# Two tokens of a head per partition for chunks 0 and 1 of a retention layer with an MLP behind it

## The chip, the core and the metric

The kernel runs on one core of one Trainium2 chip. Its time is the device time of one execution in microseconds (us); several runs are made and the median is given. The core has five engines that run their own instruction lists in order and wait for each other through semaphores: PE (matrix products, with a separate queue of weight loads, PEld), DVE (vector), ACT (scalar functions), POOL (GpSimd) and SP (only issues DMAs here). ACT and POOL issue DMAs too. A DMA is cut into packets that 16 DMA engines carry.

## The reference

q, k and v have 4 batches, 8 heads, 768 tokens and 64 dimensions, all float32. The first half is a linear attention with one decay per head, the second a two-layer MLP with a tanh GELU:

```python
for t in range(S):
    state = gamma * state + k[t] (outer) v[t]        # per batch and head, 64 x 64
    y[t] = scale * q[t] @ state
x = y.transpose(0, 2, 1, 3).reshape(B * S, H * D)    # 3072 x 512
out = gelu_tanh(x @ w_in) @ w_out                    # w_in 512 x 2048, w_out 2048 x 512
```

## The kernel before, in words

Tokens are cut into six chunks c of 128 (`C`), and each chunk is worked on for the four batches b. The recurrence is done chunk by chunk as matrix products in fp16:

- `load1` (L100) brings one 128 x 512 float32 tile of q, k or v for (c, b): partition = token, and along the row the 64 dimensions of each of the eight heads, so that a row is eight packets of 256 bytes. `prep1` (L184) turns it into fp16, q and k times a decay.
- `mm_T`/`ev_T` (L222, L234): PE transposes q and k of a head pair (eight 128 x 128 transposes), ACT or DVE copies them out of PSUM as `qkT`.
- `mm_A`/`ev_A` (L247, L261): scores A = k q^T, eight products of 64 x 128 tiles, two of them at a time in the upper and lower half of the array; DVE multiplies two 128 x 512 banks with `mask` and writes `a_sb` in fp16.
- `mm_yc`, `mm_yi`, `ev_Y` (L268, L285, L298): y from the old state `st` (64 x 64 tiles, none in chunk 0) plus y from A and v (128 x 64 tiles), copied to `xT`.
- `mm_s`/`ev_S` (L307, L321): k^T v (128 x 64 tiles), added to the state `st`.
- The MLP of a chunk: `moe1`/`moe1_two` (L416, L421) multiply `xT` with w_in into one of two PSUM banks "h", and ACT applies GELU. `moe1_two` makes two of the 16 blocks of 128 hidden columns for part of the tokens (t0 to t1). For chunk 0 the second layer is `moe2` (L432); from chunk 1 on it is `units_w` (L518), which works with sums of the weights (`w_sums`, L469) and of the hidden values (`g_sums`, L476).

PSUM has eight banks: two with tag "h", two "o" and four "att" (L217), each taken in turn. Weights come by POOL's DMA queue (`load_w_in` L378, `load_w_out` L386), in four parts each, and are converted to fp16 on the way.

The order of everything is written out by hand. From L607 stands the opening: the loads (issued from SP and ACT, L134 to L144, L607, L608, L615), products of zeros (`spin`, L153) that fill PE's waiting, and the attention of chunk 0 for batches 0 to 2, before the first MLP product (L662, `moe1_two(0, 0, *t01)`, for the tokens of batches 0 and 1). POOL's list is: the k preparations, w_in part 0, k of batch 2, w_in parts 1 to 3, k and q of batch 3, w_out (L611 to L638). Chunk 1's loads are held back by two small POOL copies (`hold`, L683 and L689), which write into the tile that the load will fill. Then `run` (L714) interleaves the 16 units of the second layer of chunk 0 with the attention of chunk 1, and the next `run` (L734) the first layer of chunk 1 with the rest of it; the number before each entry is the unit after which it is issued. Chunk 2's loads (`load(2)`, L733, 16 DMAs for q alone, L113) stand on SP behind the output stores of batches 0 to 2 of chunk 0, which `ev_O` (L447) issues.

Of the kernel before, what the change touches and what calls it, by code (L numbers as in the profile page):

```python
# [9 lines left out]
F16 = mybir.dt.float16  # L10
F32 = mybir.dt.float32
AF = mybir.ActivationFunctionType
ALU = mybir.AluOpType
# [3 lines left out]
def kernel(  # L17
# [30 lines left out]
    cst_np = np.concatenate([qdec, kdec, gst, tri], axis=1).astype(np.float32)  # L48
# [17 lines left out]
    OQ, OK, OG, OT = 0, H, 2 * H, 2 * H + NHP  # L66
# [3 lines left out]
    cst = const.tile([128, 192], F32)  # L70
# [34 lines left out]

    def load_blk(nm, c):
# [27 lines left out]
    nc.sync.dma_start(out=cst[:, :OT + 128], in_=cst_h.ap())  # L134
    load1(nc.scalar, "q", 0, 0)
    load1(nc.sync, "k", 0, 0)
    load1(nc.scalar, "v", 0, 0)
    nc.sync.dma_start(out=iden, in_=iden_h.ap())
    load1(nc.sync, "q", 0, 1)
    load1(nc.scalar, "k", 0, 1)  # L140
    load1(nc.sync, "v", 0, 1)
    load1(nc.sync, "k", 0, 2)
    load1(nc.sync, "q", 0, 3)
    load1(nc.sync, "v", 0, 3)  # L144
# [19 lines left out]
    mask = const.tile([128, 2, NHP, 128], F32, name="mask")  # L164
    for j in range(2):
        for hp in range(NHP):
            nc.vector.tensor_scalar(
                out=mask[:, j, hp],
                in0=cst[:, OT:OT + 128],
                scalar1=float(1.0 / g128[2 * hp + j]),  # L170
                scalar2=None,
                op0=ALU.mult,
            )

# [9 lines left out]
    def prep1(eng, nm, c, b):  # L184
# [14 lines left out]
        h16[nm, c, b] = t  # L199

# [46 lines left out]
    def mm_A(c, b):  # L247
        t = qkT[c, b]
# [12 lines left out]
    def ev_A(c, b):  # L261
        ps = pss.pop(("A", c, b))
        for j in range(2):
            s = att.tile([128, NHP, 128], F16, tag=f"a{j}", name=f"a_sb{j}")
            nc.vector.tensor_tensor(out=s, in0=ps[j], in1=mask[:, j], op=ALU.mult)  # L265
            a_sb[c, b, j] = s

# [336 lines left out]
    half = 2 * C  # L604


    load1(AC, "q", 0, 2)  # L607
    load1(AC, "v", 0, 2)  # L608
    spin(14)
    prep1(VE, "q", 0, 0)  # L610
    prep1(PO, "k", 0, 0)  # L611
    prep1(AC, "v", 0, 0)
    mm_T(0, 0)
    ev_T(0, 0, AC)
    load1(AC, "k", 0, 3)  # L615
    prep1(VE, "q", 0, 1)
    prep1(PO, "k", 0, 1)
# [5 lines left out]
    prep1(AC, "v", 0, 1)  # L623
    spin(2)
    mm_yc(0, 0, "o")
    mm_yi(0, 0)
    mm_s(0, (0,), "o")
    ev_Y(0, 0, AC)
    prep1(VE, "q", 0, 2)

    load_w_in(0)
    prep1(PO, "k", 0, 2)
    for i in range(1, 4):
        load_w_in(i)
    prep1(PO, "k", 0, 3)
    prep1(PO, "q", 0, 3)
    for i in range(NO):
        load_w_out(i)  # L638
    mm_A(0, 1)
    ev_A(0, 1)  # L640
    spin(3)
    mm_T(0, 2)
    ev_T(0, 2, AC)
    spin(2)
    mm_yc(0, 1, "o")
    mm_yi(0, 1)
    mm_s(0, (1,), "o")
    ev_Y(0, 1, AC)
    prep1(AC, "v", 0, 2)
    spin(2)  # L650
    mm_A(0, 2)
    ev_A(0, 2)
    ev_S(0, (0,), AC)
    prep1(AC, "v", 0, 3)
    ev_S(0, (1,), AC)
    spin(6)
    mm_T(0, 3)
    ev_T(0, 3)


    t01, t2, t3 = (0, half), (half, half + C), (half + C, 2 * half)
    moe1_two(0, 0, *t01)  # L662
    mm_A(0, 3)
    ev_A(0, 3)
    mm_yc(0, 2, "o")
    mm_yi(0, 2)
    mm_s(0, (2,))
    ev_Y(0, 2, AC)
    moe1_two(0, 1, *t01)
    ev_S(0, (2,))  # L670
    moe1_two(0, 0, *t2)
    moe1_two(0, 1, *t2)
    mm_yc(0, 3, "o")
    mm_yi(0, 3)
    mm_s(0, (3,))
    ev_Y(0, 3)
    ev_S(0, (3,))
    moe1_two(0, 2, *t01)
    for fp in range(2):
        moe1_two(0, fp, *t3)  # L680
    moe1_two(0, 2, half, 2 * half)

    hold("q", 1, 0, w_out_sb[2][0:1, 0, 0:1])  # L683
    for fc in range(6, NF):
        moe1(0, fc)
        if fc in (8, 10):
            load1(AC, "v", 1, (fc - 8) // 2)
        if fc == 11:
            hold("q", 1, 0, g_tile(0, 10)[0:1, 0, 0:1])  # L689
# [8 lines left out]
    def preps(c, b):  # L698
        prep1(VE, "q", c, b)
        prep1(PO, "k", c, b)  # L700
        prep1(AC, "v", c, b)

    load1(SY, "q", 1, 0)
    load1(SY, "k", 1, 0)
    load1(SY, "q", 1, 1)
    load1(SY, "k", 1, 1)
    load1(SY, "q", 1, 2)
    load1(SY, "k", 1, 2)
    load1(SY, "q", 1, 3)
    load1(SY, "k", 1, 3)  # L710
    load1(AC, "v", 1, 2)
    load1(AC, "v", 1, 3)
    u = [units2(0, b, tag="ooho"[b]) for b in range(B)]
    run(  # L714
        [u[i % 3][i // 3] for i in range(12)] + u[3],
        {
            1: [(w_sums, 0)],
            2: [(w_sums, 1)],
            5: [(w_sums, 2)],
            7: [(w_sums, 3)],  # L720
            8: [(preps, 1, 0)],
            10: [(att_T, 1, 0), (preps, 1, 1)],
            11: [(att_AY, 1, (), "att", 1, (0,), None)],
            12: [(att_T, 1, 1), (preps, 1, 2)],
            13: [(att_AY, 1, (0,), "h", 1, (1,), AC)],
            14: [(att_T, 1, 2), (preps, 1, 3), (att_S, 1, 0)],
            15: [(att_AY, 1, (1,), "h", 1, (2,), AC), (att_T, 1, 3), (att_S, 1, 1)],
# [9 lines left out]
            for t in ((0, half), (half, 2 * half))  # L737
# [3 lines left out]
            1: [(att_AY, 1, (2,), "o", 1, (3,), VE)],  # L741
            3: [(att_S, 1, 2), (g_sums, PO, 1, 0, 4, 0, 1)],
            4: [(att_AY, 1, (3,), "o", 1, (), VE)],
            6: [(att_S, 1, 3)],
# [89 lines left out]
```

## Time and profile before

| | before |
|---|---|
| median of 3 runs | 211.7 us (211.4 to 211.85) |
| span of the profiled execution, first to last instruction | 209.7 us, so 2.0 us of the median lie around the span |
| PE busy | 200.6 us, 96% of the span; granted clock 0.998 |
| DVE, ACT, POOL busy | 104.1, 101.9 and 115.4 us |
| DMA | 33.19 MB in 124438 packets, 117952 of them under 512 bytes |
| first MLP product of chunk 0 | 16.7 us |
| first product of the second layer of chunk 0 | 32.9 us |
| first transposes of chunk 2 | 64.8 us |

The chain of waits is read backwards from the last instruction: each piece is what the next one waited for, or what stood before it on its engine. A stretch where it names only PE is one where nothing but PE's own work counts. The timeline lists instructions with their start, duration, engine and line, and in square brackets the idle time ahead of them.

### The profile page before, as it was taken

The page shows a single profiled execution, that of the slowest core. Times are in us where ns is not written, and L with a number is a line of the kernel's source. Part 1 is how long each engine was busy: PE and PEld are TensorE (multiplying, and loading weights), DVE is VectorE, ACT ScalarE, POOL GpSimd, SP SyncE. Part 2 cuts the span into 40 slices and gives each one's busy share as a digit, 9 for nine tenths or more (in the row PEclk, how much of TensorE's full clock was granted, in tenths as well). Part 3 has the DMA queues.
Part 4 walks back from the last instruction along what each step waited for, and adds up shares of the span by engine and source line. Part 5 has one row for each costly group of instructions (what it writes and reads, how often), then busy time and mean ns, then how long its engine had stood idle before and what let it go on. Part 6 is the DMA issues. An engine that isn't in the chain of part 4 may idle for free.

```text
span 209.7 us, 4776 instructions
## 1 busy us (share of the span) xinstructions
PE 200.6 (96%) x1928; PEld 132.0 (63%) x1928; DVE 104.1 (50%) x213; ACT 101.9 (49%) x182; POOL 115.4 (55%) x120
## 2 busy tenths in 40 slices
PE   7789999999998999999999999999999999999992
PEld 3347644456786878844688744678644788545881
DVE  4445153478734649703857630867432784053430
ACT  2474563144458615168745266643365811566311
POOL 0596001133099999249998299997499980200000
PEclk9999999999999999999999999999999999999999
DMA  7999999998899798799798698796970000500004
GB/s 168 287 253 207 206 205 222 273 269 215 157 220 233 110 179 163 110 313 177 124 219 128 124 340 131 125 207 99 206 251 0 0 3 0 203 0 0 0 28 177
DMA packets 124438, 33.19 MB, mean 158 GB/s; under 512 B 117952, under 2 KB 122432, under 8 KB 124416
## 3 DMA queue, kind: packets, MB, share of 16 engines
q1 hardware_dynamic: 108272, 21.09, 50.3%
q0 software_dynamic: 5456, 8.65, 17.4%
q10 hardware_dynamic: 10688, 3.15, 6.4%
q8 instruction: 15, 0.25, 0.4%
q14 instruction: 7, 0.06, 0.1%
HBM read 30.78 MB, written 6.29 MB: 177 GB/s over the span
## 4 chain that ended last, share of the span: by engine, by line
PE 81%; SPq 6%; ACT 4%; DMA 4%; DVE 2%; issue 1%; ACTq 1%; DVEq 0%
PE h_ps L398 35%; PE o_ps L536 29%; SPq L113 5%; PE o_ps L432 5%; PE a_ps L252 3%; PE y_ps L289 3%; PE y_ps L276 2%; DMA iden<-rr_ident 2%; DMA v<-in_v_dram 2%; PE qkT_ps L229 2%; PE spin_ps L156 1%; SPq L101 1%; PE s_ps L313 1%; ACT g L414 1%; ACTq L101 1%
## 5 line engine op out<-in xcount | busy, mean ns | idle before, releaser
L398 PE MATMUL h_ps<-xT,w_in 128*128 128x512 f16 (+2 forms) x488 | 87.4, 334 | 0.5 <-ACT g L414 0.5
L414 ACT ACTIVATE g<-h_ps 128x512 f16<-128x512 f32 (+1 forms) x98 | 57.5, 589 | 33.9 <-PE h_ps L398 33.5
L398 PEld LDWEIGHTS <-w_in 128*128 128x128 f16 x488 | 45.3, 97 | 37.4 <-issue 2.8
L467 POOL TENSOR_TENSOR s_g<-g 128x512 f16<-128x512 f16 x32 | 36.9, 1152 | 9.4 <-ACT g L414 9.4
L265 DVE TENSOR_TENSOR a_sb<-a_ps,mask 128x512 f16<-128x512 f32 x48 | 30.1, 682 | 23.1 <-PE a_ps L252 23.1
L536 PEld LDWEIGHTS <-s_g 128*128 128x128 f16 x320 | 30.2, 98 | 4.3
L536 PE MATMUL o_ps<-t_w,s_g 128*128 128x256 f16 x240 | 27.8, 273 | 0.0
L536 PEld LDWEIGHTS <-g 128*128 128x128 f16 x240 | 23.4, 98 | 3.6
L467 POOL TENSOR_TENSOR s_g<-s_g,g 128x512 f16<-128x512 f16 x16 | 18.4, 1153 | 1.3
L536 PE MATMUL o_ps<-w_out,g 128*128 128x256 f16 x160 | 18.6, 273 | 0.0
L467 POOL TENSOR_TENSOR s_g<-g,s_g 128x512 f16<-128x512 f16 x16 | 18.5, 1153 | 0.0
L193 POOL TENSOR_TENSOR k<-k,cst 128x512 f16<-128x512 f32 x8 | 8.3, 1044 | 17.3 <-DMA k<-in_k_dram 17.3
L569 POOL DMA_DIRECT2D out_dram<-o_sb x8 | 5.9, 737 | 20.3 <-DVE o_sb L467 16.8
L193 POOL TENSOR_TENSOR v<-v,cst 128x512 f16<-128x512 f32 x16 | 16.2, 1044 | 0.0
L238 DVE STREAM_TRANSPOSE qkT<-kT 128x512 f16<-128x512 f16 x12 | 8.1, 678 | 15.0 <-ACT kT L180 9.5
L565 ACT COPY o_sb<-o_ps 128x512 f32<-128x512 f32 (+1 forms) x5 | 2.7, 543 | 25.1 <-PE o_ps L536 25.1
L432 PE MATMUL o_ps<-w_out,g 128*128 128x512 f16 x64 | 14.8, 380 | 0.0
L305 DVE TENSOR_TENSOR xT<-y_ps,dec 128x512 f16<-128x512 f32 x16 | 10.3, 686 | 4.5 <-PE y_ps L289 4.5
L238 DVE STREAM_TRANSPOSE qkT<-q 128x512 f16<-128x512 f16 x16 | 11.0, 690 | 2.6 <-ACT q L180 2.5
L559 ACT COPY s_u<-o_ps 128x512 f32<-128x512 f32 (+1 forms) x6 | 3.1, 514 | 17.6 <-issue 9.9
L330 DVE SCALAR_TENSOR_TENSOR st<-st,cst,s_ps 128x128 f16<-128x128 f16 (+1 forms) x40 | 10.1, 313 | 2.0 <-PE s_ps L313 2.0
L156 PE MATMUL spin_ps<-zero 128*128 128x512 f16 x32 | 9.4, 429 | 1.2 <-DVE zero L148 1.2
(55 smaller groups left out, 185.3 us busy)
## 6 DMA issues: line engine op xcount, KB each, us to landing
k<-in_k_dram SPq DMA_DIRECT2D x22, 256.0 KB, 4.7
v<-in_v_dram SPq DMA_DIRECT2D x18, 256.0 KB, 4.0
q<-in_q_dram SPq DMA_DIRECT2D x64, 64.0 KB, 2.8
out_dram<-o_sb POOLq DMA_DIRECT2D x8, 512.0 KB, 5.2
kT<-in_k_dram SPq DMA_DIRECT2D x48, 64.0 KB, 2.7
w_in<-in_moe_w_in_dram POOLq DMA_DIRECT2D x4, 512.0 KB, 9.3
w_out<-in_moe_w_out_dram POOLq DMA_DIRECT2D x4, 512.0 KB, 14.7
v<-in_v_dram ACTq DMA_DIRECT2D x6, 256.0 KB, 5.5
```

The lines of the kernel that those rows point to most:

```text
L113: nc.sync.dma_start(out=t[p0:p0 + 32, :, a, :], in_=src[j, dd, t0:t0 + 32])
L156: nc.tensor.matmul(out=ps, lhsT=zero[:, 0:128], rhs=zero, start=True, stop=True)
L193: eng.tensor_tensor(out=t, in0=src, in1=cst[:, col:col + H].unsqueeze(2).broadcast_to([128, H, Dh]), op=ALU.mult,)
L238: nc.vector.transpose(out=t[:, i].rearrange("p hp t -> p (hp t)"), in_=blk16.pop((nm, c, b)).rearrange("p ha d -> p (ha d)"),)
L265: nc.vector.tensor_tensor(out=s, in0=ps[j], in1=mask[:, j], op=ALU.mult)
L305: nc.vector.tensor_tensor(out=x, in0=ps, in1=dec, op=ALU.mult)
L330: nc.vector.scalar_tensor_tensor(out=t[:, :, hp], in0=t[:, :, hp], scalar=cst[:, OG + hp:OG + hp + 1], in1=s_ps[:, :, hp], op0=ALU.mult, o ...
L398: nc.tensor.matmul(out=out, lhsT=w_in_sb[wi][:, kc, wr * 128:(wr + 1) * 128], rhs=xT[c][:, kc, t0:t1], start=(kc == 0), stop=(kc == NHP - ...
L414: nc.scalar.activation(out=out, in_=in_, func=AF.Gelu_apprx_tanh, scale=1.0)
L432: nc.tensor.matmul(out=ps[:, n0:n1], lhsT=g_sb[c, fc // 8][:, fc % 8, b * C:(b + 1) * C], rhs=w_out_sb[fc // (NF // NO)][:, fc % (NF // NO ...
L467: eng.tensor_tensor(out=out, in0=in0, in1=in1, op=op)
L536: nc.tensor.matmul(out=po, lhsT=lhs(c, lk, fp, a), rhs=rhs(rk, fp), start=(new and fp == 0 and (last or a == 0)), stop=(stop and fp == NP ...
```

## The change

For chunks 0 and 1 (`TP`) a partition holds tokens 2p and 2p+1 of one head, with p = 0 to 63 and the heads 0 to 3 in the lower, 4 to 7 in the upper 64 partitions. A row is then four packets of 512 bytes. Each load becomes two DMAs of 64 partitions (`load2`). What follows:

- `prep2` is two instructions of 128 x 256 instead of one of 128 x 512, for q and k. A transpose now gives, per token parity r, two heads times 64 tokens.
- A, the inner part of y, and S are made of 64 x 64 tiles: 16 products where there were 8, in an order (`QUADS`) that takes the four quarters of the array in turn. The part of y from the old state keeps its number. Each result lies in two banks, by half hh.
- In chunk 1 the state part and the inner part of y write to one bank from different row halves. So `mm_yc2` ends with an ACT copy of one element (`seen`) that waits for its last product, and the first product of `mm_yi2` waits for that copy.
- `ev_Y2` and `ev_S2` are two copies each (chunk 0), by half.
- The constants `cst` grow from 148 to 424 columns (74 to 212 KB), the mask of chunks 0 and 1 is made by four instructions of 128 x 256, and the mask for the later chunks is made over by `masks` in the MLP of chunk 1.
- The opening: ACT issues only q, v of batch 0 and k of batch 1, all else is on SP; the first w_in part goes ahead of k of batch 1 on POOL, and part 1 ahead of batch 2; the first MLP product comes after batch 1; the narrow units (one batch, 128 tokens) of the first layer are eight instead of four.
- Chunk 1: one hold instead of two; attention in pairs of batches (`att2`, `att_S2`), transposes from unit 7 on; the second layer of chunk 0 runs batches 0 and 1, then 2 and 3, all in "o" banks, so that the store of batch 2 is issued after unit 14.

```diff
+    def load2(eng, nm, c, b, halves=(0, 1)):
+        t = ld_tile(nm, c, b).rearrange("p (x j) d -> p x (j d)", x=4)
+        for hh in halves:
+            eng.dma_start(
+                out=t[hh * 64:(hh + 1) * 64],
+                in_=srcs[nm][b, 4 * hh:4 * hh + 4, c * C:(c + 1) * C, :].rearrange(
+                    "h (p r) d -> p h (r d)", r=2
+                ),
+            )
...
-    nc.sync.dma_start(out=cst[:, :OT + 128], in_=cst_h.ap())
-    load1(nc.scalar, "q", 0, 0)
...
+    load2(nc.scalar, "q", 0, 0)
+    nc.sync.dma_start(out=cst, in_=cst_h.ap())
+    load2(nc.sync, "k", 0, 0)
+    load2(nc.scalar, "v", 0, 0)
     nc.sync.dma_start(out=iden, in_=iden_h.ap())
+    load2(nc.scalar, "k", 0, 1)
+    load2(nc.sync, "q", 0, 1)
+    load2(nc.sync, "v", 0, 1)
+    for nm in "kqv":
+        load2(nc.sync, nm, 0, 2)
+    for nm in "kqv":
+        load2(nc.sync, nm, 0, 3)
...
+    QUADS = [(x, r, j, hh) for x in range(2) for r in range(2) for j in range(2) for hh in range(2)]
...
+    def mm_A2(c, b):
+        t = qkT[c, b]
+        ps = [bank("att", name=f"a_ps{j}") for j in range(2)]
+        for x, r, j, hh in QUADS:
+            nc.tensor.matmul(
+                out=ps[j][half(hh), 2 * x + r],
+                lhsT=t[half(j), 1, 2 * x + r, half(hh)],
+                rhs=t[half(j), 0, 2 * x:2 * x + 2, half(hh)],
+                start=True,
+                stop=True,
+            )
...
+    def mm_yc2(c, bs, tag):
+        ys = [bank(tag, shape=(128, len(bs), 2, 128), name=f"y_ps{hh}") for hh in range(2)]
...
+        seen = nc.scalar.copy(out=misc[0:1, 1:2], in_=ys[1][0:1, len(bs) - 1, 1, 0:1])
+        needs(seen, ins)
+        yc_last[c, bs] = seen
...
+    def mm_yi2(c, bs):
...
+            for x, r, j, hh in QUADS:
+                ins = nc.tensor.matmul(
+                    out=ys[hh][half(j), i, x],
+                    lhsT=h16["v", c, b][half(hh), 4 * x + 2 * j + r],
+                    rhs=a_sb[c, b, j][half(hh), 2 * x + r],
...
+                if behind is not None:
+                    needs(ins, behind)
...
+    def mm_s2(c, bs, ss=None):
+        if ss is None:
+            ss = [bank("att", shape=(128, len(bs), 2, 64), name=f"s_ps{hh}") for hh in range(2)]
...
+    def att2(c, bs, tag, ca, abs_, engs):
+        if bs:
+            mm_yc2(c, bs, tag)
+        for b in abs_:
+            mm_A(ca, b)
+        if bs:
+            mm_yi2(c, bs)
+            ev_Y2(c, bs, engs)
+        for b in abs_:
+            ev_A(ca, b)
...
+    def ys_mm(b):
+        zs = [bank("o", shape=(128, 512), name=f"z_ps{hh}") for hh in range(2)]
...
+        mm_s2(0, (b,), ss)
+        mm_yi2(0, (b,))
...
     spin(14)
+    prep2(VE, "q", 0, 0)
+    prep2(PO, "k", 0, 0)
+    load_w_in(0)
+    prep2(PO, "k", 0, 1)
+    prep2(AC, "v", 0, 0)
     mm_T(0, 0)
+    prep2(VE, "q", 0, 1)
+    ev_T(0, 0, VE)
     spin(3)
     mm_A(0, 0)
     ev_A(0, 0)
     mm_T(0, 1)
     ev_T(0, 1, AC)
+    spin(3)
+    ys_mm(0)
+    prep2(AC, "v", 0, 1)
+    load_w_in(1)
+    prep2(PO, "k", 0, 2)
+    prep2(PO, "q", 0, 2)
+    ev_Y2(0, (0,), (AC, AC))
+    ev_S2(0, (0,), AC)
+    spin(3)
+    mm_A(0, 1)
+    ev_A(0, 1)
+    mm_T(0, 2)
+    ev_T(0, 2, AC)
+    spin(3)
+    ys_mm(1)
+    load_w_in(2)
+    prep2(PO, "k", 0, 3)
+    prep2(PO, "q", 0, 3)
+    load_w_in(3)
     for i in range(NO):
         load_w_out(i)
+    ev_Y2(0, (1,), (AC, AC))
+    prep2(AC, "v", 0, 2)
...
+    moe1_two(0, 0, *t01)
     mm_A(0, 2)
     ev_A(0, 2)
+    ev_S2(0, (1,), VE)
+    moe1_two(0, 1, *t01)
     mm_T(0, 3)
+    ev_T(0, 3, VE)
+    prep2(AC, "v", 0, 3)
+    ys_mm(2)
+    ev_Y2(0, (2,), (AC, VE))
+    moe1_two(0, 2, *t01)
     mm_A(0, 3)
     ev_A(0, 3)
+    ev_S2(0, (2,), AC)
+    moe1_two(0, 3, *t01)
+    for fp in range(3):
+        moe1_two(0, fp, *t2)
+    ys_mm(3)
+    ev_Y2(0, (3,), (AC, VE))
+    ev_S2(0, (3,), VE)
+    moe1_two(0, 3, *t2)
+    for fp in range(4):
         moe1_two(0, fp, *t3)
...
-        [u[i % 3][i // 3] for i in range(12)] + u[3],
+        [u[b][i] for b0 in (0, 2) for i in range(4) for b in (b0, b0 + 1)],
         {
...
+            2: [(w_sums, 2)],
+            4: [(w_sums, 3)],
+            5: [(preps, 1, 0)],
+            7: [(att_T, 1, 0), (preps, 1, 1)],
+            9: [(att_T, 1, 1), (preps, 1, 2)],
+            10: [(att2, 1, (), "h", 1, (0, 1), None)],
+            11: [(att_T, 1, 2), (preps, 1, 3)],
+            13: [(att_T, 1, 3)],
+            14: [(att2, 1, (0, 1), "h", 1, (2, 3), (AC, VE))],
+            15: [(att_S2, 1, (0, 1))],
...
+            1: [(att2, 1, (2, 3), "o", 1, (), (VE, AC))],
+            3: [(att_S2, 1, (2, 3)), (g_sums, PO, 1, 0, 4, 0, 1)],
+            5: [(masks,)],
```

## The prediction

> **What bounds the kernel now.** The page first:
>
> ```profile
> PE 200.6 (96%) x1928; PEld 132.0 (63%) x1928; DVE 104.1 (50%) x213; ACT 101.9 (49%) x182; POOL 115.4 (55%) x120
> ...
> DMA  7999999998899798799798698796970000500004
> GB/s 168 287 253 207 206 205 222 273 269 215 157 220 233 110 179 163 110 313 177 124 219 128 124 340 131 125 207 99 206 251 0 0 3 0 203 0 0 0 28 177
> ```
>
> PE is busy for all but 9 us. The DMA engines are full from the second slice (5.2 us) to 45 us. Next the chain of waits, in order of time (start, us, what):
>
> ```profile
> 10.60 0.33 PE a_ps L252 x8
> 10.93 0.75 PE spin_ps L156 x3
> ...
> 13.18 0.50 ACT xT L180
> ...
> 14.90 1.40 PE spin_ps L156 x6
> 16.30 0.45 PE qkT_ps L229 x8
> 16.75 1.02 PE h_ps L398 x8
> ...
> 19.58 0.60 ACT g L414
> ...
> 22.32 0.60 ACT g L414
> ...
> 22.97 10.11 PE h_ps L398 x56
> 33.08 9.50 PE o_ps L432 x44
> ```
>
> Until 16.7 us the attention of the first batches runs at the pace of loads, ACT and DVE, and products of zeros fill PE. From there on PE alone counts: it stands still for 0.8 us at the two ACT pieces (0.4 us each between the products), 0.6 us ahead of the first transposes of chunk 2 (64.8 us), and hardly elsewhere. So there are two places to gain: an earlier first MLP product, and less PE work. There is much room to lose, because every new wait of PE behind 16.7 us counts in full.
>
> Why 16.7? The timeline of the opening (start, us, engine, line, operation, idle before):
>
> ```profile
> 7.87 1.04 POOL L193 TENSOR_TENSOR k<-k,cst 128x512 f16<-128x512 f32 x1 [1.24 <-DMA k<-in_k_dram]
> 8.75 1.29 DVE L265 TENSOR_TENSOR a_sb<-a_ps,mask 128x512 f16<-128x512 f32 x2 [0.86 <-PE a_ps L252]
> 8.85 0.92 POOL L379 DMA_DIRECT2D w_in<-in_moe_w_in_dram  x1
> ...
> 14.90 1.06 POOL L193 TENSOR_TENSOR q<-q,cst 128x512 f16<-128x512 f32 x1
> ```
>
> xT of batches 0 and 1 is ready at 13.7 (the ACT piece at 13.18). But w_in part 0, issued at 8.85, takes 7.8 us to land (the shortest of its four in the table of DMA issues), so 16.65; q of batch 3 is prepared at 15.96 and its transposes stand ahead too. In the trace's packet records the first packet of w_in starts at 13.1, when ACT's queue of loads has run dry.
>
> **Loads of chunk 0.** From 4 to 12 us the queues carry 283 to 289 GB/s, nearly all 256-byte packets. The packet records show 18.0 ns for 256 bytes and 84 ns for 2048 (chunk 0's stores). A line through both gives 27.4 ns for 512 bytes, so 288 x 36/27.4 = 378 GB/s (estimate). A half load writes 64 partitions, which no row shows; the nearest are the 64 KB loads of L113 to 32 partitions, at one per 0.53 us (128-byte packets), 124 GB/s. So 124 to 378; I take 340, near the upper end, since a 256-byte packet is nearer to 512 than L113's. Up to q of batch 1 there are 5 loads of 262 KB, cst 217 (74 before) and iden 33: 1.56 MB, from 1.8 us on, the first 0.5 us at 200 GB/s, so 6.6 us, and 0.6 us until DVE can start (as for q of batch 1 before): 7.2, as before (7.20). The bigger cst eats what the packets give.
>
> A page speaks against the change. The Trainium skill, "SBUF — State Buffer", section "Door 1: The DMA port swizzle (why [64,N] ≈ [32,N])", says that a transfer to 64 partitions reaches 8 of 16 ports and carries 196 to 218 GB/s, and that two such transfers side by side gain 6%. By that the 3.15 MB of chunk 0 would take 14.4 us instead of 10.9; no run here shows it.
>
> **First MLP product.** DVE: q of batch 1 7.2 to 7.9, then the copy of the transposes that was ACT's (0.69 on DVE, 1.0 on ACT): 8.6; before 8.26. A: 8.6 to 9.0; two mask products 1.29: 10.4. ACT copies the transposes of batch 1 from 9.6 to 10.6. y and S: 10.5 to 11.0; three zeros 0.7 (row 10.93); A of batch 1 11.7 to 12.0; masks to 13.5; y to 14.0; two ACT copies of 128x256 (0.38, as GELU's): **14.8**. In the same time w_in part 0: k of batch 0 lands at about 5.1 (5.58 before), its preparation 1.04, issue at 6.2, and 7.8 us as before: 14.0. It doesn't bind then. Gain 16.7 - 14.8 = 1.9 us, bounds 0 and 2.8 (chain pieces without the zeros).
>
> **From there to the second layer** (32.9 before, 16.2 us). The MLP itself is the same work: PE starts narrow products 56 ns apart, 216 ns for four times as many columns. But the transposes of batch 3 (0.45) and A of batch 2 (0.33), once ahead of 16.7, now stand behind. Each of A, y and S of chunk 0 has a change of tile shape on either side. In the trace's single records the step between the last product of one shape and the first of the next is 0.10 to 0.12 us longer; I count 0.11. One more there: 0.1. New waits: (1) y and S of batch 2 need both "o" banks, and DVE frees them with `ev_S2` of batch 1 behind the two masks of batch 2: A ends 1.3 us after the start of this part, masks 1.29, two copies about 0.55: 3.2, PE is there at 2.6: 0.6 us. (2) Eight narrow units of 0.45 us against GELU's 0.38 plus some 0.3 us of hand-over in two banks, after wide ones with 0.60: 0.4 at the first, as now, and about 0.6 over the rest. Sum 16.2 - 0.8 + 0.9 + 1.6 = 17.9 us. The second layer starts at 14.8 + 17.9 = 32.7: **-0.2 us**. The gain is handed back.
>
> **64x64 tiles.** The records show two-tile shapes (L252, L289, L276) starting pairs 3 ns apart, and the pairs 56 ns apart (128 columns); S pairs 32 ns. Four tiles at a time: 16 products in four steps of 56, as 8 in four pairs before: no cost. If only two go together, A, inner y and S of a batch cost 0.22 + 0.22 + 0.13 us more, over eight batches 4.6, some 3.4 of it behind 14.8. No row shows four; I take four, since rows and columns each pair freely. What is saved is shape changes: 25 in chunk 1 before, by the chain's order (A, y, S per batch), 10 after: 15 x 0.11 = **-1.65 us**.
>
> **New waits in chunk 1.**
> - Transposes of batch 3 (after unit 13) need q of batch 3, and DVE's list from the transposes of batch 1 on is copy, q, four masks, copy, q: 0.6 + 0.65 + 2.45 + 0.6 + 0.65 and 0.3 of hand-over, 5.25 us (rows: two masks 1.29, copy to next 0.60). PE's work in between is four units of 0.86, A 0.55, transposes 0.46: 4.45. **+0.8** (0.4 to 1.2).
> - S of batches 0 and 1 needs two "att" banks; all four hold A of batches 2 and 3, and DVE first copies y (0.6), then masks batch 2 (1.3), from 0.25 us after y: 2.15. PE comes at 0.97 (one unit). **+1.2** (0 to 1.3).
> - `seen`: the first has 0.45 us of A as cover and stands behind ACT's copy of o_ps (0.58): 0 to 0.1. The second stands behind a GELU (0.60) that starts when the unit ends, with only the 0.55 us of state products as cover: 0.25 + 0.6 + 0.2 + 0.05 - 0.55 = **+0.5** (an element costs ACT 0.20). Behind it in ACT's queue are one y copy and GELUs with slack.
> - SP: the store of batch 2 now waits for unit 14, about 50 us instead of 44; dec and the 16 q loads (10.6 us, 46.83 to 57.42 now) end near 62 and land near 64, when ACT wants them (63.1 before). That fits only because of the waits above; they share the time, so 0 here, up to 1.3.
> - `masks` is 1.17 us on DVE, which idles there: 0.
>
> Sum of chunk 1: -1.65 + 0.8 + 1.2 + 0.5 = +0.85, with -0.2 it is **+0.65 us**. Chunks 2 to 5 keep their work. The span would be 210.4; the 2.0 us between span (209.7) and median stay: 211.7 + 0.65 = **212.3**.
>
> **Rivals.**
> 1. *Faster.* DVE's waits vanish: bank and list order as I read them cost 1.0 instead of 2.6 us in chunk 1 and 0.8 less in the opening, loads near 378 GB/s start the MLP 0.3 us earlier: 212.3 - 1.6 - 0.8 - 0.3 = 209.6; half of it gives 211.0. For it: PE has next to no such gaps now. Against: the order of the lists is fixed, and DVE was already busy 4.43 of the 5 us from 45 to 50. 36%: 209.4 to 211.2.
> 2. *Clearly slower: w_in against the loads.* w_in now goes out at 6.2 while SP still has five to seven loads to bring, all in one queue. From 31 to 34 us the trace shows w_out beside ACT's v loads: packets one for one, about 150 per us of each, so a half-kilobyte queue gets 77 GB/s, 3.4 us per load. If w_in starts at 8.5 instead of with the queue dry, k and q of batch 3 are ready near 18 to 20, and their transposes stand in PE's list at 17: +1.5 to +3; with loads at some 200 GB/s, inside the bounds above, also batch 2 is late, +4 to +9. It decides from a load rate under about 280 GB/s or a w_in delay under 3 us. 22%: 213.5 to 219, middle 215.5.
> 3. *No gain in rate*: 512-byte packets at 288 GB/s delay q of batch 1 and everything to 14.8 by about 0.9 us: 213.2, inside my own case's upper part.
>
> **How the numbers follow.** Own case 42% (211.3 to 213.5, value 212.3), rival 1 36%, rival 2 22%. About 0.2% (0.4 us) is what a measurement tells from no change: faster is under 211.3, slower over 212.1. Same: the lower third of my case, 14%; slower 28 + 22 = 50%; faster 36%. The range leaves out the fastest tenth (under 209.8) and the slowest tenth (over 216.5); my own case alone is 211.3 to 213.5.
>
> **What would show it.** Right: first h_ps near 14.8, first o_ps of L630 near 32.7, PE gaps ahead of S (L424, about 1.2) and of the last transposes of chunk 1 (0.8) with DVE as releaser, 16 products of 64x64 in the time of 8. Wrong: GB/s in the second slice not over 290, the first h_ps waiting for w_in, a gap ahead of batch 3's transposes in the opening, A products starting 28 ns apart instead of 14.

## The result, and the profile after

The changed kernel takes 236.2 us (median of 4 runs, 233.0 to 236.9) against 211.8 for the kernel before on the same chip (4 runs, 211.4 to 213.8): a ratio of 1.107, 95% interval 1.098 to 1.117. The forecast was 212.3, its range 209.8 to 216.5. Some executions of a kernel run longer at a lower granted clock, and the ratios in this document leave those out while the medians in us do not, so that for e4 and e13 below the ratio goes with 218.3 and 226.3 us. The profiled execution has a span of 234.2 us, 24.5 more than before.

The page of the changed kernel, the rows that answer to those shown of before:

```profile
span 234.2 us, 5251 instructions
PE 209.9 (90%) x2138; PEld 136.3 (58%) x2138; DVE 109.3 (47%) x218; ACT 102.6 (44%) x190; POOL 118.0 (50%) x130
...
PEclk9857999958999999999999999997799999999999
DMA  6999799696077997989988989989983000040004
GB/s 169 210 229 235 114 196 177 196 224 184 4 186 113 195 217 92 179 138 273 190 125 164 164 236 202 136 169 160 139 166 148 3 0 3 0 179 3 0 0 179
```

PE has 24 us without work, 9 before. Where before the rate was 287 and 253 GB/s in the second and third slice it is now 210 and 229, and the granted clock falls in three places: in the opening, near 50 us and near 160 us. Those are the three places where PE waits. The chain of waits, in order of time (start, us, what), names the first two:

```profile
3.89 5.12 DMA q<-in_q_dram
...
12.75 8.57 DMA k<-in_k_dram
...
26.00 12.23 DMA w_out<-in_moe_w_out_dram
...
50.31 0.60 ACTq L124
50.96 0.60 ACT g L612
51.61 2.31 PE o_ps L630 x5
```

Before, the chain was PE from 22.97 us on; here it is loads, their issues and POOL up to 51. At 50.3 it shows something else: ACT issues a load, and only then the GELU that PE waits for. The last line shows a second price of a wait: five products in 2.31 us, 462 ns each (they start 427 ns apart), where the row shown of before has 44 in 9.50 (216 ns). Around the waits of PE the trace has its clock granted at half: from 10.3 to 20.5 us, from 47.8 to 54.7 and from 160.5 to 167.3. Not every long wait does this: in e8 below PE waits 3.3 us for one load and keeps its full clock.

The first product times on PE cut both executions into stages (us; the last column is what the forecast added for the stage):

| stage | before | after | change | forecast |
|---|---|---|---|---|
| start to first MLP product | 16.7 | 21.3 | +4.5 | -1.9 |
| to the second layer of chunk 0 | 16.2 | 18.4 | +2.2 | +1.7 |
| to the first MLP product of chunk 1 | 19.0 | 28.5 | +9.5 | +0.85, with the next row |
| to the first transposes of chunk 2 | 12.9 | 13.1 | +0.2 | in the row above |
| to the last product | 140.6 | 149.1 | +8.4 | 0 |

**The opening.** From the timeline of the changed kernel (start, us, engine, line, operation, idle before):

```profile
7.81 0.92 POOL L577 DMA_DIRECT2D w_in<-in_moe_w_in_dram  x1
...
10.21 1.22 POOL L252 TENSOR_TENSOR k<-k,cst 128x256 f16<-128x256 f32 x2 [1.48 <-DMA k<-in_k_dram]
...
14.61 1.18 POOL L252 TENSOR_TENSOR k<-k,cst 128x256 f16<-128x256 f32 x2 [2.42 <-DMA k<-in_k_dram]
16.62 1.18 POOL L252 TENSOR_TENSOR q<-q,cst 128x256 f16<-128x256 f32 x2 [0.83 <-DMA q<-in_q_dram]
```

Everything waits for loads: k of batch 1 is taken up at 10.2 (7.9 before), q of batch 2 at 16.6. By the packet records w_in part 0 starts near 9.8, and from 11 to 13 us, in half microseconds, it moves 130 to 203 GB/s while the loads of q, k, v move 6 to 78. The transposes of batch 2 stand ahead of the first MLP product on PE; they start at 17.3, when POOL has prepared the first half of q.

**Chunk 1.** What ACT waited for between 30 and 60 us in the changed kernel (us in total, times, longest):

```profile
ACT g L612 <- DMA q<-in_q_dram: 9.4, 1, 9.4
...
ACT g L612 <- DMA k<-in_k_dram: 2.2, 1, 2.2
```

Its list around the longer one (timeline of the changed kernel):

```profile
38.11 0.60 ACT L612 ACTIVATE g<-h_ps 128x512 f16<-128x512 f32 x1 [0.27 <-PE h_ps L596]
45.94 2.15 ACTq L124 DMA_DIRECT2D v<-in_v_dram  x2
48.14 0.60 ACT L612 ACTIVATE g<-h_ps 128x512 f16<-128x512 f32 x1 [9.44 <-DMA q<-in_q_dram]
```

A GELU reads nothing that a load brings. But the v loads of chunk 1 stand in ACT's list ahead of the last two GELUs, and their issue waits: the program has eight completion semaphores for the DMAs of SP and ACT, given out in turn, and an issue waits until the earlier DMA with its semaphore has landed. Those earlier ones are SP's q and k loads: the issue at 45.94 has the semaphore of the k load that SP issued at 42.67 and that landed at 45.92.

**The end.** SP's list before, then after, around the first loads of chunk 2 (L113, L138):

```profile
46.83 10.59 SPq L113 DMA_DIRECT2D q<-in_q_dram  x16
```

```profile
55.38 9.83 SPq L653 DMA_DIRECT2D out_dram<-o_sb  x3
...
65.78 9.71 SPq L138 DMA_DIRECT2D q<-in_q_dram  x16
```

The third store waits for unit 14, and with it all later loads: they start 15.5 us ahead of chunk 2's first transposes, before it was 18.0. SP then issues with no gap over 0.5 us up to kT of chunk 4 (128.6 to 140.7 us) and never makes it up. There was next to no room in that list: before, this kT landed at 119.8, 0.9 us ahead of its use. From the first of these loads to that landing it was 73.0 us before and 77.5 now; why the list itself takes longer is not shown. At chunk 4 POOL pays, and PE behind it (the timeline after; before, POOL began the same casts at 120.7 with no wait):

```profile
143.44 2.28 POOL L222 CAST kT<-kT 128x512 f16<-128x512 f32 x4 [6.24 <-DMA kT<-in_k_dram]
...
161.83 2.53 PE L734 MATMUL o_ps<-t_w,s_g 128*128 128x256 f16 x11 [4.16 <-POOL s_g L665]
```

### The profile page after: what moved, and what is told of

Its sections match the earlier page's. It is cut to its first block, busy times and chain, and to the rows that moved or that the text cites. A ratio compares the mean times of both kernels' runs of the same rounds, so it can differ in the third digit from the quotient of the medians.

```text
span 234.2 us, 5251 instructions
## 1 busy us (share of the span) xinstructions
PE 209.9 (90%) x2138; PEld 136.3 (58%) x2138; DVE 109.3 (47%) x218; ACT 102.6 (44%) x190; POOL 118.0 (50%) x130
## 4 chain that ended last, share of the span: by engine, by line
PE 62%; DMA 14%; POOL 10%; SPq 4%; DVE 3%; ACT 3%; issue 1%; ACTq 0%; POOLq 0%; DVEq 0%
PE h_ps L596 26%; PE o_ps L734 26%; POOL s_g L665 8%; DMA k<-in_k_dram 5%; DMA w_out<-in_moe_w_out_dram 5%; SPq L124 4%; DMA q<-in_q_dram 4%; PE o_ps L630 2%; PE y_ps L487 2%; PE y_ps L474 2%; DVE a_sb L329 1%; PE a_ps L315 1%; PE qkT_ps L290 1%; ACT g L612 1%; PE s_ps L511 1%
## 5 line engine op out<-in xcount | busy, mean ns | idle before, releaser
L596 PEld LDWEIGHTS <-w_in 128*128 128x128 f16 x512 | 46.6, 98 | 38.4 <-issue 4.2
L734 PEld LDWEIGHTS <-s_g 128*128 128x128 f16 x320 | 31.2, 101 | 11.3 <-POOL s_g L665 6.1
L734 PE MATMUL o_ps<-t_w,s_g 128*128 128x256 f16 x240 | 30.4, 287 | 5.6 <-POOL s_g L665 5.6
L734 PEld LDWEIGHTS <-g 128*128 128x128 f16 x240 | 23.4, 98 | 3.6
L630 PE MATMUL o_ps<-w_out,g 128*128 128x512 f16 x64 | 16.6, 402 | 6.2 <-ACT g L612 5.6
L252 POOL TENSOR_TENSOR k<-k,cst 128x256 f16<-128x256 f32 x16 | 9.8, 627 | 24.5 <-DMA k<-in_k_dram 24.5
L665 POOL TENSOR_TENSOR s_g<-s_g,g 128x512 f16<-128x512 f16 x16 | 18.4, 1153 | 1.3
L767 POOL DMA_DIRECT2D out_dram<-o_sb x8 | 5.9, 737 | 17.3 <-DVE o_sb L665 14.0
L630 PEld LDWEIGHTS <-g 128*128 128x128 f16 x64 | 6.1, 101 | 13.8 <-ACT g L612 6.6
L222 DVE COPY qkT<-qkT_ps 128x1024 f16<-128x1024 f16 (+1 forms) x10 | 5.8, 578 | 14.9 <-PE qkT_ps L290 14.9
L220 ACT CAST q<-q 128x512 f16<-128x512 f32 x16 | 9.5, 618 | 6.8 <-DMA q<-in_q_dram 3.7
L503 DVE TENSOR_TENSOR xT<-y_ps,dec 128x512 f16<-128x512 f32 x16 | 10.3, 686 | 4.5 <-PE y_ps L487 4.5
L182 PE MATMUL spin_ps<-zero 128*128 128x512 f16 x26 | 11.2, 596 | 1.2 <-DVE zero L174 1.2
```

Of the source, the lines that this page charges most:

```text
L182: nc.tensor.matmul(out=ps, lhsT=zero[:, 0:128], rhs=zero, start=True, stop=True)
L220: eng.copy(out=out, in_=in_)
L252: eng.tensor_tensor(out=t[:, 4 * x:4 * x + 4].rearrange("p (r j) d -> p j r d", r=2), in0=src[:, 4 * x:4 * x + 4].rearrange("p (j r) d -> ...
L503: nc.vector.tensor_tensor(out=x, in0=ps, in1=dec, op=ALU.mult)
L596: nc.tensor.matmul(out=out, lhsT=w_in_sb[wi][:, kc, wr * 128:(wr + 1) * 128], rhs=xT[c][:, kc, t0:t1], start=(kc == 0), stop=(kc == NHP - ...
L630: nc.tensor.matmul(out=ps[:, n0:n1], lhsT=g_sb[c, fc // 8][:, fc % 8, b * C:(b + 1) * C], rhs=w_out_sb[fc // (NF // NO)][:, fc % (NF // NO ...
```

## The experiments

Theories: **T1**, a load to 64 partitions is slow to write. **T2**, twice as many loads share eight completions. **T3**, w_in takes the queues from the loads. **T4**, SP's list is late behind the third store. **T5**, tiles and list order cost something of their own. **T6** was formed on the way: the issue of a load is what is slow. Each ratio is to the kernel before, run beside it, with its interval. The runs were made on four chips, where the kernel before took 211.8 to 213.0 us, so a difference between runs of two chips can be off by about 1 us. Waits of PE are taken from the starts of its products: the step to the next one, less its usual length.

**Load shape in the changed kernel.** `e1` takes two loads of 128 partitions with two columns each, `e2` one with all four (in the code below, a step and a slice of 4). They bring other data, four heads of 256 tokens in place of eight heads of 128, so that e1, e2 and the runs built on e2 (e8, e14, e15) do not compute the layer; only their time is read.

```diff
+        src = srcs[nm][b, 4 * c:4 * c + 4, 0:2 * C, :].rearrange("h (p r) d -> p h (r d)", r=2)
+        for s in range(0, 4, 2):
+            eng.dma_start(out=t[:, s:s + 2], in_=src[:, s:s + 2])
```

> The changed kernel, with the two loads of a tensor each over all 128 partitions and two of its four 512-byte columns, instead of over 64 partitions and all four. Number (two), size (128 KB) and packet size (512 bytes) of the loads stay, and so do order, waits and all work on the engines. The data are others (four heads of 256 tokens in place of eight heads of 128), so what is computed is not the reference; read for its time alone. Theory T1, a load to 64 partitions is slow (about 215 GB/s against 288): the lateness goes; loads of the opening at 280 GB/s or more, first MLP product at 15 to 17.5 us, transposes of chunk 2 at 64 to 67, time 211.5 to 215. Theory T2, the number of loads (eight completions in turn, twice as many of half the size): nothing changes, 234 to 237. Theory T3, w_in beside the loads: the first MLP product stays over 19 us, time 216 to 230.

> As the run with two wide loads, but one load of 256 KB per tensor, 128 partitions, 512-byte packets (other data, as there). T1: the same as the two wide loads, within 1 us. T2: only here the loss goes, 211.5 to 215 against 234 to 237 there. T3: first MLP product over 19 us in both.

Measured: e1 231.9 us, 1.090 (1.083 to 1.096); e2 227.7, 1.068 (1.061 to 1.074). Neither theory alone: full width brings 4, the smaller number another 4, and most of the loss stays. The gain lies in chunk 1, whose stretch of 28.5 us falls to 23.6 and 20.7. Up to the second layer neither gains (39.6 us in the changed kernel, 41.3 in e1, 40.2 in e2): e2's first MLP product comes at 16.0, but PE then waits for batch 3.

**Load shape in the kernel before.** `e3` cuts its loads by tokens, `e4` by heads:

```diff
+                eng.dma_start(out=t[64 * s:64 * s + 64], in_=src[64 * s:64 * s + 64])
```
```diff
+                eng.dma_start(out=t[:, 4 * s:4 * s + 4], in_=src[:, 4 * s:4 * s + 4])
```

> The kernel before, each load of q, k, v of chunks 0 and 1 cut into two of 64 partitions (tokens 0 to 63, 64 to 127), 256-byte packets as before. T1: the loads of chunk 0 fall from 288 to about 215 GB/s, first MLP product 3 to 4 us later, chunk 1 late as in the changed kernel: 218 to 232. T2: as slow as the run with two loads of four heads each, whatever that is. If both are 211 to 213, the slow loads belong to 512-byte packets and not to half loads.

> The kernel before, each load of q, k, v of chunks 0 and 1 cut into two of all 128 partitions and four heads each, 256-byte packets. T1: no change, 211 to 213. T2: the issue of each load waits for the one eight before it, of half the size: 216 to 232, as slow as the run with half partitions.

Measured: e3 225.0, 1.056 (1.050 to 1.062); e4 220.5, 1.025 (1.017 to 1.034). The old layout, with 256-byte packets, loses 12 us by nothing but half loads, and about half of that by their number alone. So 512-byte packets are not needed for a loss. But it is lost elsewhere: the first MLP product comes at 28.0 in e3 and 23.1 in e4 (16.7 before), and from the second layer on both run as before to 0.2 us, with chunk 1's half loads at 210 GB/s in e3. In e3's opening the loads still carry 247 GB/s from 3 to 12 us (280 before, to 9.5); what comes late is ACT's first conversion of v, at 12.0 instead of 6.7, behind ACT's own issues, and PE waits 5.5 us for the copy behind it. Windows of the changed kernel, of e1 and of e2 show why the load shape counts in chunk 1 (from:to, us, then busy times, clock, DMA share, GB/s; the stretches are loads of chunk 0 and of chunk 1):

```profile
3.00:9.50 6.50, 5.61 (x22) 2.04 (x20) 1.90 (x6) 2.00 (x3) 2.31 (x3) 1.00 1.03 223
40.00:50.00 10.00, 6.02 (x27) 2.36 (x24) 2.28 (x6) 0.60 (x1) 2.36 (x4) 0.89 0.73 201
```
```profile
39.00:47.00 8.00, 8.00 (x39) 3.58 (x37) 3.02 (x6) 1.78 (x4) 3.70 (x6) 1.00 0.82 230
```
```profile
3.00:9.50 6.50, 4.70 (x22) 1.81 (x20) 3.09 (x8) 1.44 (x3) 3.48 (x6) 1.00 1.16 298
38.00:46.00 8.00, 8.00 (x39) 3.63 (x37) 2.19 (x6) 2.26 (x5) 2.36 (x4) 1.00 0.97 277
```

In chunk 1 the rate falls 277, 230, 201, and the DMA share falls with it, 0.97, 0.82, 0.73: the engines are not slower, they have nothing to do. By the packet records a packet takes 27 ns (median) in all three. In the opening it is not so: there the share is 1.03 in the changed kernel, and from 8 to 10 us its packets take 39 to 45 ns. What fits chunk 1 is SP's own pace. Its very first loads have nothing ahead to wait for; SP's first k loads in the changed kernel, in e1 and in e2:

```profile
1.12 1.43 SPq L124 DMA_DIRECT2D k<-in_k_dram  x2
```
```profile
1.14 1.00 SPq L125 DMA_DIRECT2D k<-in_k_dram  x2
```
```profile
1.12 0.49 SPq L125 DMA_DIRECT2D k<-in_k_dram  x1
```

Two half loads take 1.43 us to issue, e1's two 1.00, e2's one 0.49. So an issue costs 0.5 us for 128 partitions, whether 128 or 256 KB, and about 0.66 for 64 (from one to the next in chunk 1). 131 KB per 0.66 us is 198 GB/s. That is T6.

**Order of the lists.** `e5` (T4), `e6` (T2) and `e7` (T3), each one edit:

```diff
-        eng = nc.sync if b < B - 1 else nc.gpsimd
+        eng = nc.sync if b < B - 2 else nc.gpsimd
```
```diff
-            load2(AC, "v", 1, fc - 13)
...
+        for b in (b0, b0 + 1):
+            load2(SY, "v", 1, b)
```
```diff
+    prep2(PO, "k", 0, 1)
     load_w_in(0)
-    prep2(PO, "k", 0, 1)
...
+    prep2(PO, "k", 0, 2)
+    prep2(PO, "q", 0, 2)
     load_w_in(1)
```

> The changed kernel with one edit: the store of batch 2 of chunk 0 goes out on POOL's queue, as that of batch 3 does, so that SP goes on to the loads of chunk 2 without waiting for unit 14. Theory T4 (SP's list of loads, put behind that store, runs late up to chunk 4 and makes POOL and PE wait at 157 to 166 us): the loads of chunk 2 start near 57 instead of 65.8 us, POOL's casts of kT of chunk 4 wait for nothing, the two gaps of PE ahead of chunk 3's second layer (1.6 and 4.3 us) and the slower clock behind them go, 8 us less: 227 to 229. If the late second half is only the opening's lateness carried on (T1), nothing changes: 235 to 237.

> The changed kernel with one edit: the loads of v of chunk 1 leave ACT's list and go out on SP, behind q and k of the same two batches. Theory T2 (a load's issue waits for the landing of the eighth load before it, and ACT's GELUs stood behind such an issue): the gaps of 3.6 and 2.6 us at 48.8 and 51.6 go, and the stretch from the first second-layer product of chunk 0 to the first product of chunk 1's MLP falls from 28.5 to about 23 to 25 us; time 231 to 233.5. Theory T1 (the loads of chunk 1 are late by their rate whoever issues them): PE waits in their place ahead of the transposes of batches 2 and 3 or ahead of y, the stretch stays at 27 us or more; 235 to 237.

> The changed kernel with one edit: in POOL's list w_in part 0 goes out behind the preparation of k of batch 1, and part 1 behind those of k and q of batch 2. Theory T3 (w_in takes the queues from the loads): q and k of batches 2 and 3 are ready 1 to 3 us earlier, the transposes of batch 3 too; the first MLP product stays at 20 to 22 us (part 0 now lands at about 19), and the second layer starts 1 to 2 us earlier: 233.5 to 235.5. T1 and T2 (the loads' own rate): the loads go at 215 GB/s with or without w_in beside them, within 0.7 us of 236.2, or slower if part 0 now comes too late.

Measured: e5 228.4, 1.074 (1.065 to 1.083): T4 holds, 7.8 us (7.0 by the ratios). The last stage takes 140.6 us, as before. The loads of chunk 2 no longer stand behind unit 14, and POOL's casts are there in time; this is the timeline of e5:

```profile
136.77 2.28 POOL L222 CAST kT<-kT 128x512 f16<-128x512 f32 x4
```

e6 230.4, 1.085 (1.076 to 1.094): the stretch of 28.5 us falls to 22.7, 5.8 us, by moving the issues of v out of ACT's list (eight, of which four stood ahead of GELUs), at the same rate of loads (200 GB/s from 41 to 55 us). So most of the loss in chunk 1 was who stood behind the loads; their rate by itself leaves some 2 us, as e2's stretch is 20.7.

e7 235.1, 1.103 (1.093 to 1.113), not told apart from the changed kernel. Its profile shows both halves of T3: the attention is ready some 4 us before the first MLP product, which now waits for w_in. The second layer starts at 43.0, 3.3 us later than in the changed kernel, and the stretch of chunk 1 behind it gives half of that back.

```profile
20.35 1.89 PE L596 MATMUL h_ps<-xT,w_in 128*128 128x256 f16 x8 [3.98 <-DMA w_in<-in_moe_w_in_dram]
```

The opening has more to load by then than the queues bring; the order only chooses who waits.

**All undone at once.** `e8` is e2 with the edits of e5 and e7.

> The run with one wide load of 256 KB per tensor (other data, as there), together with the store of batch 2 on POOL and w_in later. It asks what is left of the loss when load shape, order of SP and order of w_in are undone and the tiles, the order of chunk 1 and the waits on banks stay. T1 to T4 together: 227.7 less 7.2 (end) less 4 to 7 (v of batch 3, which landed at 23.1 us beside w_in) is 213.5 to 216.5. If the tiles or the re-planned list cost something more of their own (T5): over 218.

Measured: 217.4, 1.022 (1.014 to 1.029), 1 us over what T1 to T4 gave. Of the 18.9 us that this takes back, the load shape is 8.6 (e2), order the rest. What is left against before, by stages: 1.7 to the first MLP product (w_in again: PE has nothing else from 15.1 on and waits 3.3 us for it), 2.1 to the second layer, 2.5 up to chunk 2, nothing behind. The 2.1 and the 2.5 are put down to T5 as what is left; no run undoes the tiles.

**Issue or transfer.** `e9` issues first halves on SP, second halves on ACT; `e10` makes four loads of one 512-byte column over 128 partitions:

```diff
+            load2(SY, nm, 1, b, (0,))
+            load2(AC, nm, 1, b, (1,))
```
```diff
+        src = srcs[nm][b, :, c * C:(c + 1) * C, :].rearrange("(hh x) (p r) d -> x hh p (r d)", hh=2, r=2)
+        for x in range(4):
+            eng.dma_start(out=t[:, x], in_=src[x])
```

> The changed kernel with one edit: in chunk 1 every tensor's first half is issued by SP and its second half by ACT, all of ACT's behind the last GELU of chunk 0. Theory T6, formed on the first eight runs: what is slow is not the transfer but its issue, 0.66 us of a queue for each half of 128 KB (198 GB/s from one queue), against 0.49 us for a load of 128 partitions of 128 or 256 KB. Then two queues side by side carry more than 260 GB/s, the last load of chunk 1 lands near 51 instead of 55 us, and the stretch from the first second-layer product to the first product of chunk 1's MLP falls from 28.5 to about 21.5 to 22.7 us: 229 to 231. Theory T1, 64 partitions are slow to write: halves side by side stay at 200 to 235 GB/s, the loads end at 53 us or later and the stretch is 23 us or more: 231 to 233.5.

> The changed kernel, each tensor loaded by four loads of 64 KB over all 128 partitions (one 512-byte column each) instead of two halves; the data stand as in the changed kernel. T6: each issue takes 0.49 us, so a queue carries 64 KB per 0.51 us, 129 GB/s, less than with halves: loads of chunk 0 end 5 us later or more, chunk 1's too, time 242 to 260. T1: faster than the changed kernel, as the run with two wide loads: 229 to 233.

Measured: e9 238.0, 1.119 (1.111 to 1.128), a miss on both sides. ACT's first issue came at 45.2, when SP's twelve were nearly out, since its completion semaphore stood behind SP's. So the two queues ran side by side for a few microseconds only. But that separates three cases; windows of e9: SP's first halves alone, both queues, ACT's second halves alone.

```profile
42.00:45.00 3.00, 3.00 (x15) 1.35 (x14) 0.27 (x1) 0.00 (x0) 0.00 (x0) 1.00 0.79 193
48.00:50.00 2.00, 0.09 (x2) 0.09 (x2) 0.57 (x2) 0.00 (x0) 0.00 (x0) 0.73 1.22 246
51.00:55.00 4.00, 0.79 (x4) 0.36 (x5) 1.36 (x3) 0.89 (x2) 1.85 (x3) 0.50 1.24 179
```

The issues of the first of these stretches (timeline of e9):

```profile
42.24 0.61 SPq L124 DMA_DIRECT2D v<-in_v_dram  x1
42.91 0.61 SPq L124 DMA_DIRECT2D q<-in_q_dram  x1
```

SP alone: 193 GB/s at a share of 0.79 and 27 ns a packet, with an issue every 0.66 us; that is T6. ACT alone, with a backlog of issued loads into one half of the partitions: the engines full (1.24, as in the opening of the kernel before at 280 GB/s) and still only 179 GB/s, 54 ns a packet. That is T1. Both halves at once: 246 GB/s, 39 ns. So both theories hold, and they meet near 200 GB/s. T6 is what limits chunk 1's loads in the changed kernel; in its opening, where the share is 1.03 and SP and ACT both issue, packets are slow for a part of the time, as in T1. The Trainium skill, "SBUF — State Buffer", section "Door 1: The DMA port swizzle (why [64,N] ≈ [32,N])", gives 196 to 218 GB/s for a load to 64 partitions, and the section "Can I just issue two DMAs to hit both halves?" behind it 6% more for two side by side; measured here are 179, and 246 for both halves, 37% more.

e10: 352.5, 1.660 (1.650 to 1.670), far outside both. SP's list in e10:

```profile
1.14 6.72 SPq L127 DMA_DIRECT2D k<-in_k_dram  x4
...
10.99 10.24 SPq L127 DMA_DIRECT2D q<-in_q_dram  x4
```

A 64 KB load takes 1.7 us to issue at first and 2.6 later; from 3 to 12 us the queues carry 45 GB/s at a DMA share of 0.16. So the run says nothing on T1: something else holds all loads on few of the sixteen engines (0.16 of 16 is 2.6). The Trainium skill, "DMA: Bandwidth & Descriptors", section "Why a DMA increments its semaphore by 16 and not by 1", says that a DMA runs on the largest number of engines, up to 16, that divides the outermost dimension of both sides. The source's outermost dimension here is 2. Two engines with a 512-byte packet per 27 ns each would carry 38 GB/s (estimate from that rule and the packet time), near the 45; no run here changes that dimension alone.

**Do the losses add up?** `e11` is e9 with the store of e5, `e13` is e6 with the store of e5.

> The changed kernel with halves on two queues in chunk 1 and the store of batch 2 on POOL. If the two losses are separate they add up: about 6 for ACT and the loads of chunk 1, 7.8 for the end, so 221.5 to 224. If the late list of SP is only what the late chunk 1 made of it, one of them brings nothing: 228 to 231.

> The changed kernel with v of chunk 1 loaded on SP and the store of batch 2 on POOL's queue. If the two losses are separate: 236.2 less 5.8 less 7.8 is 222.6, 221.5 to 224. If SP's list, now longer by the v loads, is late again: 226 to 230.

Measured: e11 230.2, 1.085 (1.078 to 1.091): the store brings its 7.8 us on top of e9 (238.0), the two queues bring nothing. e13 227.2 (224.9 to 230.8 over four runs), 1.067 (1.059 to 1.076), against 222.6 if they added up. In its profiled run they nearly do (224.9; 24.0 us in chunk 1's stretch), but PE again waits 1.9 us for POOL in chunk 3's second layer, and POOL 2.4 us for kT of chunk 4. SP's loads of chunk 2 start 19.0 us ahead of the transposes there, more than before, so why that kT is late again is not shown.

**The wait for the att banks.** `e12` (on e11) and `e14` (on e8) move S of batches 0 and 1:

```diff
-            15: [(att_S2, 1, (0, 1))],
...
+            0: [(att_S2, 1, (0, 1))],
             1: [(att2, 1, (2, 3), "o", 1, (), (VE, AC))],
```

> The run with halves on two queues and the store on POOL, and besides S of batches 0 and 1 of chunk 1 behind the first unit of chunk 1's MLP instead of ahead of it. The wait for two att banks that DVE's masks free (1.3 to 1.7 us in the records) goes, since a unit of 1.9 us covers it: 1.0 to 1.7 us faster than that run. If PE only meets the next wait on DVE (y of batches 2 and 3, xT), less than 0.4 us.

> The run with wide loads (other data), store on POOL and w_in later, and besides S of batches 0 and 1 of chunk 1 behind the first unit of chunk 1's MLP. The wait for two att banks (1.1 and 0.6 us in the records of that run, of which 0.4 is S itself) goes: 1.0 to 1.5 us faster than 217.4, 215.8 to 216.5. If DVE's list is the limit all the same (y of batches 2 and 3, or xT, wait in its place): within 0.4 us of 217.4.

Measured: e12 228.8, 1.078 (1.072 to 1.084); e14 216.6, 1.020 (1.015 to 1.025). Neither is told apart from its base by the time. In the profiles the wait goes (e14: 0.4 us left of 1.7; the stretch from the second layer to chunk 2 falls from 34.3 to 32.7), in e12 the wait goes too, but that stretch is 42.5 us beside 42.1 in e11: PE waits for the late loads instead.

**w_in early or late.** `e15` is e2 with the store of e5 and only w_in part 1 later. `e16` is the kernel before with w_in part 0 ahead of k of batch 1.

> Wide loads (other data) and the store on POOL; w_in part 0 early, as in the changed kernel, and only part 1 behind k and q of batch 2. Against the run with both parts later (217.4, first product at 18.4 with 3.3 us of waiting for w_in) and the one with both early (227.7 less 7.2 for the store, 220.5; first product at 15.95, then 4.6 us of waiting for batch 3). T3, w_in takes the queues packet for packet: first product near 16 again, half of the waiting for batch 3: 215.5 to 219. If the early part 0 alone holds v of batch 3 back to 23 us: 220 to 221.5.

> The kernel before with one edit: w_in part 0 goes out ahead of the preparation of k of batch 1, some 2 us earlier. T3: its packets of 2 KB then share the queues with the loads of batches 2 and 3, whose preparation comes 1 to 2 us later, and the transposes of batch 3 wait: 0.5 to 2 us slower, 212.5 to 214. If w_in only lands earlier: the first product moves from 16.7 to 16.0 to 16.5, 211.0 to 211.8.

Measured: e15 217.7, 1.026 (1.020 to 1.031), the same as e8; the first product is at 17.8 with no long wait behind it. e16 213.8, 1.008 (1.006 to 1.011): T3 in the kernel before. Its timeline:

```profile
6.72 0.92 POOL L379 DMA_DIRECT2D w_in<-in_moe_w_in_dram  x1
...
16.44 1.04 POOL L193 TENSOR_TENSOR k<-k,cst 128x512 f16<-128x512 f32 x1 [2.23 <-DMA k<-in_k_dram]
...
18.54 0.40 PE L229 MATMUL qkT_ps<-iden,q 128*128 128x128 f16 x4 [1.81 <-POOL q L193]
```

2.1 us earlier for w_in make k of batch 3 2.6 us later, and with it the first MLP product (19.0, before 16.7). (The packet records give w_in's packets 1 KB, the expectation 2.) No run is faster than the kernel before.

## Why the prediction was wrong, point by point

- **"So 124 to 378; I take 340": the step that failed.** Measured: 223 GB/s in the opening, 201 in chunk 1. The row that I put at the lower end (one 64 KB load per 0.53 us) held the price of an issue, which is much the same for loads of 128 and 256 KB. 131 KB per 0.53 us is 247 GB/s, under the 280 below which rival 2 saw w_in and the loads collide. I divided bytes by packet times and never by issues. And even over 128 partitions 512-byte packets carried 298 (e2), not 378: my line through two packet times overstates what longer packets bring. The page on 64 partitions, which I showed as speaking against the change and took into no number, was nearer, in chunk 1 by luck: there the issues set the 201 GB/s, and only e9's window with a backlog shows what a half of the partitions takes. By itself this step is worth the 8.6 us of e2. That overlaps with the third step named below, since e2's stretch of chunk 1 is short with v still on ACT.
- **First MLP product 14.8.** With wide loads it comes at 16.0 (e2), 0.8 ahead of before instead of 1.9: q of batch 1 is taken up at 8.3 instead of 7.2, and from there it is 7.7 us, where I had 7.6, so the chain on the engines was worked out rightly. With half loads q of batch 1 is taken up at 9.6, the transposes of batch 2 wait for their q as well, and the product comes at 21.3.
- **Opening to second layer, 17.9:** measured 18.4 after, 18.3 in e8. Near, 0.4 to 0.5 too small; 24.3 in e2, where batch 3 is late.
- **Tiles four at a time:** right, the 16 products of A start 14 ns apart on average, where the 8 of before started 26 ns apart. The shape changes, taken as what is left: e8's stretch from the second layer to chunk 2 is 2.5 us longer with 3.8 us of waits in it, so 1.3 saved, where I had 1.65.
- **Waits of chunk 1:** transposes 0.8, measured 0.85 in e8; S 1.2, measured 1.3 (after) and 1.7 (e8); `seen` 0.5, measured 0.46. One was missed: PE's third MLP unit, which reads batches 0 and 1 of `xT`, waits 0.8 us for the copies of batches 2 and 3 into the same tile.
- **"SP: 0 here, up to 1.3", the second step: wrong by 7.8 us (e5).** I compared SP's list with the moment when ACT wants chunk 2's q, and stopped there. The list runs on for 75 us with no gap over 0.5 us, and its next date with little slack is kT of chunk 4. "Chunks 2 to 5 keep their work" is true of the work and not of the order.
- **ACT's issues, the third step:** no term at all, that is nothing, without a reason; 5.8 us (e6). I asked what stands behind waiting instructions on DVE, PE and SP, and not behind ACT's own DMA issues.
- **Rival 2** had the mechanism and the place (e7, e16) and even the loads at 200 GB/s. It was too small, because it ended with the opening; the measured time lies above the whole of it (213.5 to 219).
- `masks`, put at 1.17 us and nothing: it took 6.25 us, and no wait of PE behind it names DVE.

What stays open: how much of the opening's 4.5 us is the loads' rate and how much w_in, as the two are never undone apart with half loads; whether two queues from the start would carry the changed kernel's halves at 246 GB/s throughout, which the order of the completion semaphores prevented in e9 (e3's 256-byte halves, issued from both, carried 247 in its opening); and what the tiles cost by themselves.

## What to carry to other kernels

Price a DMA twice, by its bytes and by its issue: cutting a load in two costs the issuing queue a second half microsecond, and the smaller pieces may carry less than the whole however long their packets are. An engine that issues loads between its computations hands on every wait of those issues to whatever stands behind them. When a wait is put into a list that is nearly full (a store ahead of the loads), follow that list to its next date with little slack, however many stages later.

## What the runs showed of the hardware that was not expected

- An issue from SP or ACT, with nothing to wait for, took 0.4 to 0.6 us for 128 partitions (128 or 256 KB, e1, e2 and before) and 0.6 to 0.8 for 64 partitions of half the size.
- A stream into one half of the partitions filled the DMA engines (share 1.24) at 179 GB/s; both halves side by side carried 246 (e9), all 128 partitions 298 (e2).
- A long wait of PE can cost more than itself: behind the waits near 50 us five products start 427 instead of 216 ns apart (up to nine in other runs), and of the 8.4 us lost in the last stage the waits themselves are 5.9. In e8 the clock stays whole through a wait of 3.3 us.
- Eight DVE instructions of 128x128 took 6.25 us beside POOL's work on `s_g`, where the kernel before has eight in 1.17 us in its opening.
